# Loading two attention pairs before the branch, and an MLP step's activation inside attention's last steps

## The chip, the cores and the metric

The kernel runs on one core of a Trainium2 chip. The metric is the time of one execution in device microseconds. Before the change it is 683.89 us (median of 3 runs, 683.73 to 685.13).

## What is computed

Banded attention with eight global keys, then two MLPs on its output, everything in float32:

```
# attention: 2 batches, 8 heads, 768 positions, head size 64
scores = q @ k.T / 8 + bias[h]                 # bias = -slope[h] * distance
keep   = (key < n_global) | (0 <= i - key < n_local)       # 8 and 96
a = softmax(where(keep, scores, -1e9))
x = (a @ v)  reshaped to 1536 tokens x 512
# first MLP: 512 -> 2048 -> 512
h = x @ w_in
x = (h * tanh(softplus(h))) @ w_out            # mish
# second MLP: 512 -> 1536 -> 512
xn = x / rms(x) * rms_g
out = (silu(xn @ w_gate) * (xn @ w_val)) @ w_out2
```

## The kernel before

**Branch.** Ahead of the branch come the loads of the two limits, the first loads of attention, and the maps from which the bias is made. All engines then read a flag; with the limits of these inputs they go to `attention_banded`. Four tiles of `room`, which hold the MLP's sums later, hold data for the start of attention.

**Attention.** Heads are worked in pairs. A pair of a batch has 6 units, one for each 128 queries, so there are 48 units and 24 steps of two units; pair n begins with step 3n. A unit meets at most 256 keys. Its operations, with their engines: scores (TensorE, L651), a custom VectorE operation that adds the bias and reduces (L677), the exponential (ScalarE, L690), the inverse sums for two units (VectorE, L701 and L702), scaling (GpSimd, L706), transposes (TensorE, L715), their evacuation (ScalarE, L723), the product with the values (TensorE, L736), and for every third unit the split of the result into a high (ScalarE, L355) and a low half (VectorE, L358).

**Weights.** A weight piece comes as 64-bit words into one of four `stage` tiles (512 KiB; L129). Seven operations make its two halves: `mag` (L161), `clamp` (L167), `b1` (L170), `b2` (L176), `b3` (L182) on VectorE, `hi` and `lo` on GpSimd for the six early pieces (L193, L201), on ScalarE and VectorE for later ones. `mag` of piece i asks for the loads up to piece i, `b3` of piece i for those up to piece i + 3. Pieces 0 to 3 are `w_in`, 4 to 7 `w_out`, 8 and 9 `w_in` again.

**The plan.** In attention each operation has a due time in steps: its step plus the offset in `AT`. The offsets are: scores 0, reduction 0.95 and 1.44, exponential 1.36 and 1.68, inverse sums 2.2, scaling 2.71 and 3.16, transposes 3.29, evacuation 3.87, values 4.65, high split 5.15, low split 5.77 (first and second unit of a step). A piece's operations are due at `CONV_AT[k]` plus the offsets in `AT_CONV`, or `AT_LATE` for pieces 4 and 5. The work of each engine is sorted by due time, and every engine executes its list in this order. A step that stands ahead of another on its engine holds it up. SP issues all DMAs in order as well, except for four loads of the first values, which ScalarE's queue issues.

**Attention's data.** Pair 0 lies in `room` tiles: queries and keys in two halves, values in two halves. Pairs from 1 on go to a pool with two buffers each for queries, keys and values; pair n's load waits for the last use of pair n - 2.

**MLP 1.** It has 32 steps s. A step makes two chunks of 128 hidden columns for 384 tokens: 24 products (L367), then mish: `tanh` of each chunk (L387), a table load and two functions (`cosine`, L391 to L393), `times` (VectorE, L396), a high split (L493) and a low split (L497). The sums of a step (18 products with `w_out`, L419) are put off into `pend` and issued by `flush(0)` of the next step's mish, behind the next step's products. The first four chunks (`ahead`) are multiplied among attention's last steps; `mish1(0, ...)` follows attention, `mish1(1, ...)` opens `mlps`. Each mish also handles the weight pieces begun by the one before; `begin(2)` at the end of the first starts pieces 6 and 7, five VectorE operations each.

Of the kernel before, what the change touches and what calls it, by code (L numbers as in the profile page):

```python
# [17 lines left out]
P = 128  # L18
B, H, S, D = 2, 8, 768, 64
NT = S // P  # L20
# [6 lines left out]
TB = BT // P  # L27
# [22 lines left out]
CONV_AT = (3.0, 7.0, 11.0, 14.5, 21.2, 22.2)  # L50
# [10 lines left out]
def tile_attention_mish_swiglu(  # L61
# [163 lines left out]
    q_first = room[2][:, 0:S]  # L225
    k_first, v_first = (
        room[i][:, 0 : (2 * NT - 1) * P].rearrange("p (n c) -> p n c", c=P) for i in (3, 0)
    )
    maps = room[1]

    def tiles_v(v_t, b, p, own=slice(0, NT), queue=None):


        queue = queue or sp
        vp = v[b][:, p * P : (p + 1) * P]
        vr = vp.rearrange("(t r) e -> r t e", r=P)
        queue.dma_start(v_t[:, own, :], vr[:, own, :])
        n, last = max(own.start - 1, 0), own.stop - 1
        win = slice(NT + n, NT + last)
        for r in (slice(GLOBAL_MAX, 64), slice(64, P)):  # L240
            queue.dma_start(v_t[r, win, :], vr[r, n:last, :])  # L241
        queue.dma_start(
            v_t[0:GLOBAL_MAX, win, :],
            vp[0:GLOBAL_MAX].rearrange("r (o e) -> r o e", o=1).to_broadcast(
                (GLOBAL_MAX, last - n, P)
            ),
        )

    for m in range(2):
        tok = slice(m * BT, (m + 1) * BT)  # L250
        own, win = slice(m * TB, (m + 1) * TB), slice(NT + (m and 2), NT + 2 + 3 * m)
        sp.dma_start(q_first[:, tok], qT[0, 0][:, tok])
        sp.dma_start(k_first[:, own, :], kT[0, 0][:, own, :])
        sp.dma_start(k_first[:, win, :], kT[0, 0][:, win, :])
# [11 lines left out]
    tiles_v(v_first, 0, 0, slice(0, TB), act)  # L266
# [235 lines left out]
    def mish1(s, mish):  # L502

        blk, cs = s // 2 % NBLK, chunks(s)
# [21 lines left out]
        begin(BEGUN1[s])  # L526

# [64 lines left out]
    def attention_banded():  # L592
        fresh()
        mm = [mm_bank() for _ in range(4)]
        with ExitStack() as st:
# [15 lines left out]
            def load_v(b, p):  # L611
                v_t = qk.tile([P, 2 * NT - 1, P], F32, tag="v", name=nm("v"))
                tiles_v(v_t, b, p)
                vs[b, p] = v_t

            qs[0, 0], ks[0, 0], vs[0, 0] = q_first, k_first, v_first
            load_qk(0, 1)
            tiles_v(vs[0, 0], 0, 0, slice(TB, NT))
            sp.dma_start(gcol, rms_g)
            conv_prefetch(2)  # L620

# [177 lines left out]
            for h in range(2, H):  # L799
                add("DVE", 1.5 * h - 1.3, ("BIAS", h), [("BIAS", h - 1)],  # L800
                    lambda h=h: make_bias(h))
            for n in range(2, B * NPAIR):
                add("SP", 3 * n - 3.9, ("LOADQK", n), [("QK", NT * (n - 1) - 1)],
# [197 lines left out]
```

## Time and profile before

| | |
|---|---|
| median of 3 runs | 683.89 us |
| the profiled execution | 687.29 us |
| its span | 685.5 us |
| TensorE busy in the span | 660.5 us (96%) |
| VectorE | 448.6 us (65%) |
| ScalarE | 379.5 us (55%) |
| GpSimd | 65.5 us (10%) |

The profile is of one execution. The busy time of TensorE includes matmuls at a lower granted clock, so a busy slice is not yet a fast one; its clock has two levels, 2.4 GHz (shown as 1.00) and 1.2 GHz (0.50). A line of the timeline gives the start, the duration, engine, source line, operation, the tiles, the count, and in brackets how long the engine was idle before it and what ended that. The idle time of an engine that is not the bottleneck costs nothing.

### The profile page before, as it was taken

The numbers are of one execution on the slowest core, as the hardware profiler recorded it, in microseconds if no ns is written. First come the engines' busy times: TensorE is split into PE (matmuls) and PEld (weight loads), VectorE is DVE, ScalarE is ACT, GpSimd is POOL, SyncE is SP. The second block draws the span as 40 slices with busy tenths as digits, with TensorE's granted clock in tenths as the row PEclk, the third lists the DMA queues.
The fourth block names the chain that finished last, engine by engine and source line by source line (L and its number), as shares of the span: only waits on it lengthen the run. The fifth ranks groups of instructions, "written<-read, shape, count | busy, mean of one in ns | idle before, by whom it ended". The sixth has DMA issues, their size and how long they took to land.

```text
span 685.5 us, 9837 instructions
## 1 busy us (share of the span) xinstructions
PE 660.5 (96%) x3712; PEld 589.5 (86%) x3712; DVE 448.6 (65%) x1029; ACT 379.5 (55%) x716; POOL 65.5 (10%) x124
## 2 busy tenths in 40 slices
PE   6979997999999999999999999999999999999996
PEld 3657786999999999999878999999999999999995
DVE  4768857887788778877777787882467873232222
ACT  3969968888888888888888322321122221111211
POOL 1547870000000000000000000000000000000000
PEclk9798998999999999999999999999999999999999
DMA  7775632222212212221112122221013200010011
GB/s 232 218 235 180 204 103 63 92 93 65 71 63 92 80 63 68 86 62 63 62 62 62 45 79 94 80 74 32 1 61 99 87 1 0 1 47 12 35 47 51
DMA packets 26727, 54.19 MB, mean 79 GB/s; under 512 B 2608, under 2 KB 14640, under 8 KB 26672
## 3 DMA queue, kind: packets, MB, share of 16 engines
q1 hardware_dynamic: 25968, 53.16, 24.3%
q8 instruction: 31, 0.51, 0.3%
q10 hardware_dynamic: 704, 0.33, 0.2%
q14 instruction: 24, 0.20, 0.1%
HBM read 50.34 MB, written 3.15 MB: 78 GB/s over the span
## 4 chain that ended last, share of the span: by engine, by line
PE 85%; ACT 5%; DVE 5%; DMA 2%; issue 1%; SPq 1%; DVEq 0%; POOL 0%; POOLq 0%
PE mm L367 45%; PE s L419 31%; PE s L736 3%; PE s L715 3%; PE mm L651 3%; DMA stage<-in_w_in_dram 2%; DVE x L431 1%; ACT junk L465 1%; DVE d L396 1%; ACT e L690 1%; ACT L391 1%; ACT L387 1%; PE s L448 1%; SPq L241 0%; DMA lim_i<-in_n_global_dram 0%
## 5 line engine op out<-in xcount | busy, mean ns | idle before, releaser
L367 PE MATMUL mm<-hl,w 128*128 128x384 f32 x1920 | 349.4, 336 | 0.0
L367 PEld LDWEIGHTS mm<-hl,w 128*128 128x128 f32 x1920 | 336.8, 188 | 7.1 <-issue 0.5
L419 PE MATMUL s<-w,g 128*128 128x512 f32 x1008 | 249.2, 397 | 6.8 <-issue 5.0
L419 PEld LDWEIGHTS s<-w,g 128*128 128x128 f32 x1008 | 188.6, 190 | 45.2 <-issue 5.2
L557 ACT ACTIVATE r<-mm 128x384 f32<-128x384 f32 x48 | 23.5, 490 | 128.6 <-PE mm L367 128.6
L558 DVE TENSOR_TENSOR r<-r,mm 128x384 f32<-128x384 f32 x48 | 26.4, 549 | 65.9 <-ACT r L557 65.9
L431 DVE TENSOR_TENSOR x<-x,s 128x512 f32<-128x512 f32 x60 | 40.2, 687 | 40.2 <-PE s L419 40.2
L493 ACT ACTIVATE g<-r 128x384 fp32r<-128x384 f32 x48 | 25.2, 525 | 71.5 <-DVE r L558 71.5
L396 DVE TENSOR_TENSOR d<-d,mm 128x384 f32<-128x384 f32 x64 | 32.5, 549 | 35.1 <-ACT d L393 35.1
L690 ACT ACTIVATE e<-e,s 128x256 f32<-128x256 f32 (+1 forms) x96 | 46.2, 502 | 11.5 <-DVE s L677 11.5
L706 POOL TENSOR_SCALAR e<-e,s 128x256 f32<-128x256 f32 (+1 forms) x96 | 47.8, 515 | 35.1 <-ACT e L690 10.7
L182 DVE SCALAR_TENSOR_TENSOR bits<-stage,bits 128x512 int32<-128x512 int32 x68 | 47.4, 697 | 2.1
L176 DVE SCALAR_TENSOR_TENSOR bits<-stage,bits 128x512 int32<-128x512 int32 x68 | 47.3, 695 | 2.1
L493 ACT ACTIVATE g<-d 128x384 fp32r<-128x384 f32 x64 | 33.5, 526 | 24.1 <-DVE d L396 22.6
L497 DVE TENSOR_TENSOR g<-r,g 128x384 fp32r<-128x384 f32 x48 | 26.8, 559 | 28.4 <-ACT g L493 28.4
L201 DVE TENSOR_TENSOR w<-bits,w 128x512 fp32r<-128x512 f32 x62 | 42.7, 688 | 0.0
L391 ACT ACT_TABLE_LOAD x32 | 41.1, 1283 | 0.6
L387 ACT ACT_TABLE_LOAD x31 | 39.8, 1283 | 0.5
L677 DVE CUSTOM_DVE_ANT_0 e<-mm,bias 128x256 f32<-128x256 f32 (+1 forms) x96 | 33.8, 392 | 8.2 <-PE s L715 7.3
L197 ACT ACTIVATE w<-bits 128x512 fp32r<-128x512 f32 x62 | 38.2, 616 | 0.0
L387 ACT ACTIVATE d<-mm 128x384 f32<-128x384 f32 x64 | 30.2, 491 | 12.0 <-PE mm L367 10.5
L161 DVE TENSOR_SCALAR bits<-stage 128x512 int32<-128x512 int32 x68 | 28.8, 424 | 11.2 <-DMA stage<-in_w_in_dram 11.2
(79 smaller groups left out, 472.4 us busy)
## 6 DMA issues: line engine op xcount, KB each, us to landing
stage<-in_w_out_dram SPq DMA_DIRECT2D x28, 512.0 KB, 3.2
stage<-in_w_in_dram SPq DMA_DIRECT2D x16, 512.0 KB, 3.9
stage<-in_w_gate_dram SPq DMA_DIRECT2D x12, 512.0 KB, 3.4
stage<-in_w_val_dram SPq DMA_DIRECT2D x12, 512.0 KB, 3.4
k<-in_kT_dram SPq DMA_DIRECT2D x7, 704.0 KB, 4.4
out_dram<-x SPq DMA_DIRECT2D x12, 256.0 KB, 2.1
q<-in_qT_dram SPq DMA_DIRECT2D x7, 384.0 KB, 5.1
v<-in_v_dram SPq DMA_DIRECT2D x7, 384.0 KB, 4.6
```

Source lines behind the costliest of these rows:

```text
L176: dve.scalar_tensor_tensor(self.bits, self.lw, 29, self.bits, op0=ALU.logical_shift_right, op1=ALU.bitwise_or,)
L182: dve.scalar_tensor_tensor(self.bits, self.hw, -1073741824, self.bits, op0=ALU.bitwise_and, op1=ALU.bitwise_or,)
L201: engine.tensor_tensor(self.wt[:, 1, :], self.fl, self.wt[:, 0, :].bitcast(F32), op=ALU.subtract)
L367: pe.matmul(ps[:, 0:BT], w[:, wi, col], xs[kc][:, xi, :], start=kc == 0 and i == 0, stop=kc == NK - 1 and i == 2,)
L387: act.activation(self.t[:, i, :], self.h[i], AF.Tanh, scale=0.5)
L391: act.preload_act_table_set("trig_and_small")
L396: dve.tensor_tensor(self.t[:, i, :], self.t[:, i, :], self.h[i], op=ALU.mult)
L419: pe.matmul(acc[m], gt[:, gi, tok], w[:, wi, :], start=c % 4 == 0 and i == 0, stop=c % 4 == 3 and i == 2,)
L431: dve.tensor_tensor(y, y, acc[m], op=ALU.add)
L493: act.activation(gt[:, 0, :], x, AF.Copy)
L690: act.activation(e, e, AF.Exp, scale=-1.0, bias=s[:, 0, u % 2, j : j + 1], accum_out=s[:, 1, u % 2, j : j + 1],)
L706: pool.tensor_scalar(e, e, es[u // 2][1][:, 3, u % 2, j : j + 1], 0.0, op0=ALU.mult, op1=ALU.add,)
```

## The change

- The loads of pair 1's queries and keys go ahead of the branch, into the `room` tiles 2 and 0. Pair 0's values go from `room` tile 0 into the pool; they are loaded whole, from SP, behind the branch. The helper `tiles_v` with its halves and its choice of queue goes away.
- The order of loads on SP behind the branch becomes: piece 0, pair 0's values, `rms_g`, pair 2's queries and keys, piece 1, pair 1's values, pieces 2 and 3. Pair 3's queries and keys are next and wait for nothing; values from pair 2 on wait for the values product of pair n - 2.
- `CONV_AT` moves the early pieces 0 to 3 later by 1.6, 1.0, 0.4 and 0.2 steps.
- Of the 16 `ahead` products, those of chunks 0 and 1 come closer together (0.12 steps apart instead of 0.23), those of chunks 2 and 3 spread over 25.0 to 27.3 steps.
- The mish of chunks 0 and 1 becomes planned work: `tanh` at 25.2 and 25.7, `cosine` at 25.95, `times` at 27.0, the splits at 27.3 and 27.5. Behind the plan come `begin(2)` for pieces 6 and 7, and `sums_later`, which puts off the sums of step 0; `mish1(1, ...)` then issues them.

```diff
--- before.py
+++ after.py
@@ -47,7 +47,7 @@
     "HI": (5.15, 5.16), "LO": (5.77, 5.66),
 }
 
-CONV_AT = (3.0, 7.0, 11.0, 14.5, 21.2, 22.2)
+CONV_AT = (4.6, 8.0, 11.4, 14.7, 21.2, 22.2)
 AT_CONV = dict(mag=-0.53, clamp=0.96, b1=3.89, b2=6.09, b3=7.15, hi=7.69, lo=8.79)
 AT_LATE = dict(mag=2.5, clamp=3.0, b1=3.4, b2=4.0, b3=4.5, hi=5.0, lo=5.5)
 
@@ -222,36 +222,20 @@
 
 
     room = [xypool.tile([P, TB * DM], F32, tag="xy", name=nm("x")) for _ in range(NBLK)]
-    q_first = room[2][:, 0:S]
-    k_first, v_first = (
+    q_first = [room[2][:, i * S : (i + 1) * S] for i in range(2)]
+    k_first = [
         room[i][:, 0 : (2 * NT - 1) * P].rearrange("p (n c) -> p n c", c=P) for i in (3, 0)
-    )
+    ]
     maps = room[1]
-
-    def tiles_v(v_t, b, p, own=slice(0, NT), queue=None):
-
-
-        queue = queue or sp
-        vp = v[b][:, p * P : (p + 1) * P]
-        vr = vp.rearrange("(t r) e -> r t e", r=P)
-        queue.dma_start(v_t[:, own, :], vr[:, own, :])
-        n, last = max(own.start - 1, 0), own.stop - 1
-        win = slice(NT + n, NT + last)
-        for r in (slice(GLOBAL_MAX, 64), slice(64, P)):
-            queue.dma_start(v_t[r, win, :], vr[r, n:last, :])
-        queue.dma_start(
-            v_t[0:GLOBAL_MAX, win, :],
-            vp[0:GLOBAL_MAX].rearrange("r (o e) -> r o e", o=1).to_broadcast(
-                (GLOBAL_MAX, last - n, P)
-            ),
-        )
 
     for m in range(2):
         tok = slice(m * BT, (m + 1) * BT)
         own, win = slice(m * TB, (m + 1) * TB), slice(NT + (m and 2), NT + 2 + 3 * m)
-        sp.dma_start(q_first[:, tok], qT[0, 0][:, tok])
-        sp.dma_start(k_first[:, own, :], kT[0, 0][:, own, :])
-        sp.dma_start(k_first[:, win, :], kT[0, 0][:, win, :])
+        sp.dma_start(q_first[0][:, tok], qT[0, 0][:, tok])
+        sp.dma_start(k_first[0][:, own, :], kT[0, 0][:, own, :])
+        sp.dma_start(k_first[0][:, win, :], kT[0, 0][:, win, :])
+    sp.dma_start(q_first[1], qT[0, 1])
+    sp.dma_start(k_first[1], kT[0, 1])
 
     small = cpool.tile([P, 28], F32, tag="small", name="small")
     half, mhalf = small[:, 0:1], small[:, 1 : 1 + TB]
@@ -263,7 +247,6 @@
     dve.memset(mhalf, -0.5)
     dve.memset(half_pi, HALF_PI)
     act.activation(primed, half, AF.Exp)
-    tiles_v(v_first, 0, 0, slice(0, TB), act)
     ones = room[1][:, 10 * P : 12 * P].bitcast(BF16)
     dve.memset(ones, 1.0)
     dve.memset(least[:, 0:1], 1.0)
@@ -501,7 +484,6 @@
 
     def mish1(s, mish):
 
-        blk, cs = s // 2 % NBLK, chunks(s)
         for i in range(2):
             mish.tanh(i)
         do_one(between)
@@ -524,6 +506,10 @@
             piece("lo")
         do_one(ends)
         begin(BEGUN1[s])
+        sums_later(s, gt)
+
+    def sums_later(s, gt):
+        blk, cs = s // 2 % NBLK, chunks(s)
 
         def later():
             def done(m):
@@ -609,15 +595,31 @@
                 qs[b, p], ks[b, p] = q_t, k_t
 
             def load_v(b, p):
+
+
                 v_t = qk.tile([P, 2 * NT - 1, P], F32, tag="v", name=nm("v"))
-                tiles_v(v_t, b, p)
+                vp = v[b][:, p * P : (p + 1) * P]
+                vr = vp.rearrange("(t r) e -> r t e", r=P)
+                sp.dma_start(v_t[:, 0:NT, :], vr)
+                for r in (slice(GLOBAL_MAX, 64), slice(64, P)):
+                    sp.dma_start(v_t[r, NT:, :], vr[r, 0 : NT - 1, :])
+                sp.dma_start(
+                    v_t[0:GLOBAL_MAX, NT:, :],
+                    vp[0:GLOBAL_MAX].rearrange("r (o e) -> r o e", o=1).to_broadcast(
+                        (GLOBAL_MAX, NT - 1, P)
+                    ),
+                )
                 vs[b, p] = v_t
 
-            qs[0, 0], ks[0, 0], vs[0, 0] = q_first, k_first, v_first
-            load_qk(0, 1)
-            tiles_v(vs[0, 0], 0, 0, slice(TB, NT))
+            for p in range(2):
+                qs[0, p], ks[0, p] = q_first[p], k_first[p]
+            conv_prefetch(1)
+            load_v(0, 0)
             sp.dma_start(gcol, rms_g)
+            load_qk(0, 2)
             conv_prefetch(2)
+            load_v(0, 1)
+            conv_prefetch(4)
 
             biases = bp.tile([P, H, 3 * P], BF16, tag="bias", name="bias")
             bias, bias0 = biases[:, :, 0 : 2 * P], biases[:, :, 2 * P :]
@@ -799,12 +801,12 @@
             for h in range(2, H):
                 add("DVE", 1.5 * h - 1.3, ("BIAS", h), [("BIAS", h - 1)],
                     lambda h=h: make_bias(h))
+            for n in range(3, B * NPAIR):
+                add("SP", 3 * n - 3.9, ("LOADQK", n),
+                    [("QK", NT * (n - 1) - 1)] if n > 3 else [],
+                    lambda n=n: load_qk(*divmod(n, NPAIR)))
             for n in range(2, B * NPAIR):
-                add("SP", 3 * n - 3.9, ("LOADQK", n), [("QK", NT * (n - 1) - 1)],
-                    lambda n=n: load_qk(*divmod(n, NPAIR)))
-            for n in range(1, B * NPAIR):
-                add("SP", 3 * n + (0.7 if n > 2 else -2.4), ("LOADV", n),
-                    [("PV", NT * (n - 1) - 1)] if n > 2 else [],
+                add("SP", 3 * n + 0.7, ("LOADV", n), [("PV", NT * (n - 1) - 1)],
                     lambda n=n: load_v(*divmod(n, NPAIR)))
             pieces = [Piece(k) for k in range(NW_EARLY)]
             for k, piece in enumerate(pieces):
@@ -813,15 +815,25 @@
                     add("POOL" if op in ("hi", "lo") else "DVE", at, (op, k),
                         [("lo", k - 3)], lambda piece=piece, op=op: piece(op))
 
+
             for j in range(4 * NK):
-                add("PE", ns - 0.1 + 0.23 * j, ("AHEAD", j),
+                add("PE", ns - 0.1 + (0.12 * j if j < 8 else 1.1 + 0.33 * (j - 8)), ("AHEAD", j),
                     [("TTR", nu - 4 + k, c) for k in range(2 + 2 * (j >= 8)) for c in range(2)]
                     + [("lo", j % NK)],
                     lambda j=j: ahead(j))
+            mish, gt = [], []
+            add("ACT", ns + 1.19, ("MISH",), [("AHEAD", 4)], lambda: mish.append(Mish(first[0:2])))
             for c in range(2):
-                add("ACT", ns + 1.3 + 0.7 * c, ("TANH", c),
-                    [("AHEAD", 4 * c + 3)], lambda c=c: mish_first[0].tanh(c))
-            mish_first = []
+                add("ACT", ns + 1.2 + 0.5 * c, ("TANH", c), [("AHEAD", 4 * c + 3)],
+                    lambda c=c: mish[0].tanh(c))
+                add("DVE", ns + 3.0 + 0.01 * c, ("TIMES", c), [("COSINE",)],
+                    lambda c=c: mish[0].times(c))
+                add("ACT", ns + 3.3 + 0.01 * c, ("HIGH", c), [("TIMES", c)],
+                    lambda c=c: gt.append(split_hi(mish[0].t[:, c, :])))
+                add("DVE", ns + 3.5 + 0.01 * c, ("LOW", c), [("HIGH", c)],
+                    lambda c=c: split_lo(gt[c], mish[0].t[:, c, :]))
+            add("ACT", ns + 1.95, ("COSINE",), [("TANH", 0), ("TANH", 1)],
+                lambda: mish[0].cosine())
 
 
             names = {w[3] for w in work}
@@ -836,13 +848,12 @@
             while any(queues.values()):
                 w = min(q[0] for q in queues.values() if q and ready(q[0]))
                 queues[w[2]].pop(0)
-                if w[3] == ("TANH", 0):
-                    mish_first.append(Mish(first))
                 w[5]()
                 done.add(w[3])
             for piece in pieces:
                 piece.rest()
-            mish1(0, mish_first[0])
+            begin(BEGUN1[0])
+            sums_later(0, gt)
         mlps(1, Mish(first[2:4]))
 
 
```

## Rows read from the trace of the kernel before

**Rows 1.** The page, part 2: busy tenths in 40 slices, and the clock.
```profile
PE   6979997999999999999999999999999999999996
...
PEclk9798998999999999999999999999999999999999
```

**Rows 2.** Chain of waits in order of time: start us, us, what; whole kernel.
```profile
11.31 5.50 DMA stage<-in_w_in_dram
...
84.94 1.06 PE mm L651 x8
...
102.75 1.02 PE s L736 x16
103.78 4.99 issue
108.77 6.74 PE s L419 x18
...
123.79 4.18 PE mm L367 x24
127.98 4.12 PE s L419 x18
```

**Rows 3.** Timeline, 11 to 25 us, TensorE's scores and transposes, VectorE's first piece.
```profile
14.32 1.18 PE L651 MATMUL mm<-k,q 64*128 64x128 f32 x8 [2.92 <-DMA q<-in_qT_dram]
...
16.83 0.43 DVE L161 TENSOR_SCALAR bits<-stage 128x512 int32<-128x512 int32 x1 [5.31 <-DMA stage<-in_w_in_dram]
...
18.78 2.42 PE L651 MATMUL mm<-k,q 64*128 64x256 f32 x8 [1.80 <-DVE s L677]
...
21.13 1.97 PE L715 MATMUL s<-ident,e 128*128 128x128 f32 x8
...
24.51 1.41 PE L651 MATMUL mm<-k,q 64*128 64x256 f32 x8
```

**Rows 4.** Pair 1's queries: issue (timeline, SP), then KB and us to landing.
```profile
6.96 0.44 SPq L608 DMA_DIRECT2D q<-in_qT_dram  x1
...
q<-in_qT_dram SPq DMA_DIRECT2D x1, 384.0 KB, 7.2
```

**Rows 5.** Stretches: engines' busy us (instructions), TensorE's clock, DMA share, GB/s.
```profile
0.00:9.00 9.00, 6.38 (x28) 2.68 (x28) 4.94 (x36) 2.94 (x9) 1.08 (x8) 1.00 0.66 182
...
4.00:6.00 2.00, 1.66 (x8) 0.61 (x7) 0.86 (x7) 0.00 (x0) 0.00 (x0) 1.00 1.05 376
9.00:25.00 16.00, 11.28 (x60) 7.49 (x58) 8.06 (x47) 10.49 (x40) 6.05 (x14) 0.68 0.98 295
...
25.00:26.00 1.00, 1.00 (x9) 0.56 (x8) 0.00 (x0) 0.79 (x4) 1.00 (x3) 0.95 0.93 182
...
30.00:42.00 12.00, 12.00 (x130) 9.19 (x126) 9.49 (x49) 12.00 (x45) 7.89 (x17) 1.00 0.46 153
```

**Rows 6.** Timeline, 36 to 71 us: scores of steps 9, 11 and 18, a piece.
```profile
36.58 0.93 PE L651 MATMUL mm<-k,q 64*128 64x128 f32 x8
...
42.17 1.13 PE L651 MATMUL mm<-k,q 64*128 64x256 f32 x8
...
46.86 0.43 DVE L161 TENSOR_SCALAR bits<-stage 128x512 int32<-128x512 int32 x1 [5.89 <-DMA stage<-in_w_in_dram]
...
70.02 0.93 PE L651 MATMUL mm<-k,q 64*128 64x128 f32 x8
```

**Rows 7.** Timeline, 94 to 127 us, ScalarE and VectorE.
```profile
94.56 1.08 ACT L723 ACTIVATE pt<-s 128x512 f32<-128x512 f32 x2 [1.36 <-PE s L715]
...
104.35 0.56 DVE L358 TENSOR_TENSOR hl<-s,hl 128x384 fp32r<-128x384 f32 x1 [3.21 <-ACT hl L355]
...
106.59 0.93 ACT L393 ACTIVATE d<-d,small 128x768 f32<-128x768 f32 x1
...
109.65 0.42 DVE L161 TENSOR_SCALAR bits<-stage 128x512 int32<-128x512 int32 x1
...
126.90 1.02 DVE L497 TENSOR_TENSOR g<-d,g 128x384 fp32r<-128x384 f32 x2
```

## Prediction

> **What bounds the kernel now.** I read the slices first, then the chain of waits, then the timeline around each place where the chain leaves TensorE. TensorE is busy in 9 tenths of nearly every slice; the thin or slow ones are the second to fourth and the one around 110 us, where the clock row shows 7 as well [rows 1]. The chain shows two holes in the first 115 us: 5.50 us for a weight stage issued at 11.31, and 4.99 us without work at 103.78, after which the first 18 sums take 6.74 us where later ones take 4.12 [rows 2]. The timeline adds a third, 5.89 us of idle VectorE up to 46.86 [rows 6]. From 113 us on the chain is TensorE's, so what is won before stays won unless a helper then falls short.
>
> Steps are counted as in the plan: step i holds units 2i and 2i+1, pair n begins with step 3n, QK(i) are the scores of step i.
>
> *Hole 1.* VectorE sits idle 5.31 us until 16.83, because `mag` of piece 0 (due 2.47) stands ahead of the reductions of step 2 (due 2.95) and its stage lands only then [rows 3]. Beside it TensorE waits 2.92 us, from 11.4 to 14.32, for pair 1's queries. QK(5) comes at 24.51.
>
> *Hole 2.* VectorE waits there for the stage of piece 2: `b3` of piece 0 (due 10.15) asks for that load only 0.32 steps ahead of `mag` of piece 2 (10.47), and the request then queues behind a load of values.
>
> *Hole 3.* The first mish's table load and its two functions on ScalarE start only behind the last high split of attention, whose low half begins at 104.35, and end at 107.52 [rows 7].
>
> The work between is ScalarE's: QK(18) at 70.02 to QK(23) at 84.94, which is 2.98 us a step [rows 2, 6].
>
> **Start of attention.** All early bytes go through one queue, so I date landings by bytes. By 9.0 us 182 GB/s x 9.0 = 1638 kB had moved, and 295 GB/s from there to 25 [rows 5]. A load lands some time after its own bytes could be through: pair 1's queries (issued 6.96, 7.2 us to landing, so 14.2 [rows 4]) end at 2556 kB of the order, when 1638 + 5.2 x 295 = 3172 kB had moved: 616 kB late. Piece 0's stage (11.31 + 5.50 = 16.8 [rows 2]) ends at 3475 kB, moved 3939: 464 kB late. I take 500 kB.
>
> The new order on SP is pair 0 (1088 KiB), pair 1 (1088), piece 0 (512), pair 0's values (704), pair 2's keys and queries (1088), piece 1 (512), pair 1's values (704), pieces 2 and 3 (1024), pair 3's keys and queries (1088). By (end + 500 - 1638)/295 + 9 they land at: pair 1 12.7, piece 0 14.5, values 0 16.9, pair 2 20.7, piece 1 22.5, values 1 24.9, pieces 2 and 3 28.5, pair 3 32.2. The first values left ACT's queue (320 KiB = 328 kB there), so SP alone may have moved up to 328 kB less by 9.0, 0 to 1.1 us; I add 0.3, because SP is blocked in that time for only some of it. Pair 1 is then there at 13.0 instead of 14.2.
>
> Now the two waits. `mag` of piece 0 goes to 4.07, behind the reductions of steps 2 and half of 3, which need the transposes of step 0. These follow QK(3), 13.0 + 1.1 + 0.9 = 15.0; the stage is there at 14.5 + 0.3 = 14.8, so the 5.31 us go. What is late next is pair 1: QK(3) at 13.0. Steps 3 to 5 then take what steps 9 to 11 take, 42.17 - 36.58 = 5.59 us [rows 6], so QK(5) stands at 18.6 instead of 24.51. The first values product comes after QK(3), transposes 0, QK(4) and transposes 1, about 1.1 each, so near 17.3; its data is there at 16.9 + 0.3 = 17.2. That cover is thin: each us later costs a us. From QK(5) to QK(9) 36.58 - 24.51 = 12.07 us, so QK(9) is due at 30.7 - but pair 3's data, now behind two more stages, lands at 32.5. ScalarE, which sets the pace, works about a step behind the scores and so takes up the first of that wait; I allow 0.7 us, an estimate between nothing and the whole. QK(9) counts as 31.8 against 36.58: **4.8 us won**; ends 3.1 (below) and 5.9 (no wait for pair 3).
>
> At this place the DMA: Bandwidth & Descriptors page of the Trainium skill ("Issuing engines are not separate DMA queues") says that a second issuing queue saves only issue time, because the same 16 engines move the bytes. The row at 4 to 6 us shows 376 GB/s with both queues feeding, the stretch with SP alone 295 [rows 5]. By the rule the 0.3 us would be nothing, and the whole 666.1.
>
> **Middle.** Four stages exist and all four are loaded by 28.5 to 28.8; `mag` of pieces 1 and 2 stand at 7.47 and 10.87 steps, about 26 and 37 us. From QK(11) at 42.17 to QK(18) at 70.02 are 27.85 us; seven steps at 2.98 are 20.9. **7.0 us won** (the 5.89 us idle, and the half clock that follows it); ends 6.0 (some of it was work caught up later) and 7.1. By the same dating pair 2's values land at 35.0 against a need at 36.7, and pair 4's keys and queries at 38.8 against QK(12) at 40.7. The other edits of the SP order (pair n's loads wait for pair n-2, as before) cost nothing by the same margins. ACT loses four DMA issues that nothing waited for.
>
> **End of attention.** From 84.94 to the last values at 102.75 the chain holds TensorE's pieces without a wait of 0.1 us (18 pieces, the first and the last in [rows 2]), and the change only reorders its work: chunks 0 and 1 move to 23.9 to 24.74 in the plan, chunks 2 and 3 spread to 27.31. The last values then end at the same distance, 103.78 on the old clock. Mish moves among them: two tanh, then table load and two functions on ScalarE (104.35 to 107.52, 3.2 us [rows 7]) between the evacuations of steps 22 and 23. The evacuation of step 22 began at 94.56; two more chunk steps (three products each, 4.18/8 = 0.5 us) now stand ahead of its transposes, so it ends near 94.6 + 1.0 + 1.1 = 96.7 or, with tanh of chunk 1 ahead of it, 97.2. The block ends at 100.4, the evacuation of step 23 at 101.5; its values begin at 102.75. That is 1.3 us of cover; were it gone, up to 1.9 us would be late. `times`, high and low splits end about 103.5. So the sums start at 103.85 with no idle and at the high clock: 4.99 + (6.74 - 4.12) = 7.6 us leave TensorE.
>
> But VectorE gives some back. It runs with no idle from 109.65 (first op of piece 6) to the low split of the third mish at 126.90 [rows 7]. In the changed kernel that run starts behind the last low split of attention, 104.35 + 0.56 = 104.91: 4.74 us earlier, not 7.6. The low split's first half ends at 126.90 + 0.55 - 4.74 = 122.7; the sums that need it (127.98 before [rows 2]) can start two matmuls (0.46) earlier, at 122.2. TensorE would be there at 103.85 + 2 x (4.12 + 4.18) = 120.5 [rows 2] and waits 1.8. **5.7 us won**; ends 4.5 (evacuations late) and 7.4 (VectorE not the limit).
>
> **Sum.** 4.8 + 7.0 + 5.7 = 17.5 us. The profiled execution took 687.29 us, its span 685.5; changed: 669.8 and 668.0. The median of the runs is 3.4 us under the profiled one; taking the same gain off it: 683.89 - 17.5 = **666.4 us**.
>
> **Rivals.** (1) *Half clock in the ramp.* Today the clock is at 1.2 GHz for most of 15 to 25 us after TensorE sat idle, back at 25.05, 6.3 us after gapless work began at 18.78 [rows 3, 5]. If QK(3) at 13.0 meets the low clock too, QK(4) costs 2.42 instead of 1.13, and two blocks of transposes (1.97 for eight at the low clock, half of that at the high one) 0.7 and 0.9 more, rounded down to 2.8 us as the clock falls late. QK(5) at 21.4, pair 3 no longer late: 3.1 won there, 668.1. For: idle from 11.4 to 13.0. Against: half as much idle as now. The TensorE: Matmul & The Clock Gate page of the Trainium skill (Part 4) says that transposes don't count as busy work for the clock in the way matmuls do; by that the ramp, a third transposes, would stay slow and the time be this rival's 668.1. The stretch from 30 to 42 us, with the same mix and no idle, is at 1.00 throughout [rows 5], so the trace doesn't bear the rule out there.
> (2) *Loads late.* With 616 kB and the full 328 kB: QK(3) 14.2, pair 3 33.8, 3.5 won, 667.7. At 250 GB/s instead of 295, pair 4 is late as well (44 us, QK(12) at 43.5 for 49.44, and 2.7 us of the later loss): 5.9 + 2.7 + 5.7 = 14.3, 669.6. For: piece 0 and values 0 now share the fullest stretch.
> (3) *The end does not do what it says*: the mish is not ready at the last values, since tanh of chunk 1 waits for eight chunk steps and ScalarE works in order. Then idle returns and only the clock part, 2.6, stays: 669.5.
> (4) *More:* no wait for pair 3, no VectorE limit: 5.9 + 7.0 + 7.4 = 20.3, 663.6.
> (5) *Slower.* TensorE stays at the low clock through attention, because small idle gaps now come evenly. A step costs 2.42 + 1.97 + about 2.0 for the values (taken as the transposes') = 6.4 us at 1.2 GHz [rows 3] against 2.98: 3.4 more. From 17.5/3.4, over five more slow steps than now, it is slower; ten more give 700. Against: all steps from 26 to 42 us were at the high clock.
>
> **How the numbers follow.** Forecast 0.50, (1) 0.15, (2) 0.14, (3) 0.08, (4) 0.09, (5) 0.04. About 0.2% (1.4 us) is what a measurement of this kernel can tell from no change. Faster 0.95; same 0.02 and slower 0.03 come out of (5). Range 662.5 to 673: from (4) less 1, to (2) and (3) together (671 to 673).
>
> **What would show it.** VectorE's first piece op with no idle over 1 us ahead of it; QK(5) at 18 to 19 us; QK(9) waiting 1 to 2 us for `k` or `q`; no wait of VectorE for a stage near 35 to 45; QK(23) near 73; L419 following the last L736 within 0.3 us at clock 1.00; then some 2 us in which the third block of sums waits for L497. Wrong would be: clock 0.50 between 13 and 20 (rival 1), the first L736 waiting for `v` (2), L736 of step 23 or L419 waiting for ScalarE (3).

## The result, and the profile of the changed kernel

| | before | after | after / before |
|---|---|---|---|
| median of 6 runs each, us | 684.80 | 668.62 | 0.9761 [0.9746, 0.9776] |
| profiled execution | 687.29 | 668.87 | |
| its span | 685.5 | 667.1 | 18.4 less |
| TensorE busy in it | 660.5 (96%) | 653.8 (98%) | |

The change takes 16.2 us off the median; 17.5 was forecast, and 666.4 us for 668.62. On the page, TensorE and its clock in 40 slices (answers [rows 1]):

```profile
PE   8999999999999999999999999999999999999996
...
PEclk9999999999999999999999999999999999999999
```

The 7s of the third slice and of the one near 110 us are gone, the first slice is an 8 for a 6, and the clock row has no slice under 9 any more (before: a 7 and two 8s [rows 1]). Where the time went is read from the timeline of TensorE (start, duration, operation, count, idle time before and what ended it), start to middle of attention:

```profile
11.61 0.93 PE L653 MATMUL mm<-x,x 64*128 64x128 f32 x8 [0.21 <-DMA x<-in_kT_dram]
...
17.05 0.44 PE L738 MATMUL s<-pt,v 128*64 128x128 f32 x4 [0.49 <-DMA v<-in_v_dram]
17.41 1.13 PE L653 MATMUL mm<-x,x 64*128 64x256 f32 x8
...
29.73 0.93 PE L653 MATMUL mm<-k,q 64*128 64x128 f32 x8 [0.44 <-DVE s L703]
...
35.30 1.13 PE L653 MATMUL mm<-k,q 64*128 64x256 f32 x8
...
56.19 0.93 PE L653 MATMUL mm<-k,q 64*128 64x128 f32 x8
...
71.12 1.14 PE L653 MATMUL mm<-k,q 64*128 64x256 f32 x8
```

These are QK(3), the first product with the values, QK(5), QK(9), QK(11), QK(18) and QK(23); L653 was L651 [rows 3, 6]. VectorE's first piece operation, 5.31 us idle in [rows 3], now has no wait in brackets:

```profile
14.00 0.66 DVE L161 TENSOR_SCALAR bits<-stage 128x512 int32<-128x512 int32 x1
```

The end of attention on TensorE: last values, then the first, second, third and fifth block of sums (L402 was L419):

```profile
89.27 1.09 PE L738 MATMUL s<-pt,v 128*64 128x128 f32 x16
90.29 4.40 PE L402 MATMUL s<-w,g 128*128 128x512 f32 x18
...
98.71 4.26 PE L402 MATMUL s<-w,g 128*128 128x512 f32 x18
...
108.29 0.73 PE L402 MATMUL s<-w,g 128*128 128x512 f32 x2 [1.13 <-ACT g L476]
109.27 3.92 PE L402 MATMUL s<-w,g 128*128 128x512 f32 x16 [0.24 <-DVE g L480]
...
125.58 0.73 PE L402 MATMUL s<-w,g 128*128 128x512 f32 x2
126.56 3.93 PE L402 MATMUL s<-w,g 128*128 128x512 f32 x16 [0.24 <-DVE g L480]
```

The 4.99 us without work and the slow 6.74 us block of [rows 2] are gone; the sums follow the values at once, at 4.40 us. The same kernel was profiled a second time with the last experiments ("again"). Starts of the same work in us, and what each profile of the changed kernel has won by then:

| | before | after | won | again | won |
|---|---|---|---|---|---|
| QK(5) | 24.51 | 17.41 | 7.1 | 18.01 | 6.5 |
| QK(11) | 42.17 | 35.30 | 6.9 | 36.67 | 5.5 |
| QK(18) | 70.02 | 56.19 | 13.8 | 57.17 | 12.9 |
| QK(23) | 84.87 | 71.12 | 13.7 | 72.09 | 12.8 |
| first sums | 108.77 | 90.29 | 18.5 | 91.26 | 17.5 |
| sixth block of sums | 152.72 | 134.51 | 18.2 | 135.45 | 17.3 |
| last block of sums | 674.91 | 656.67 | 18.2 | 657.64 | 17.3 |
| end of the span | 685.5 | 667.1 | 18.4 | 666.7 | 18.8 |

So the start won 5.5 to 6.9 us, the middle 7.0 to 7.4, the end 4.5, and behind the sixth block nothing more happens but the very end of the span.

### The profile page after: what moved, and what is told of

Read it like the earlier page. It is cut to its first block, busy times and chain, and to the rows that moved or that the text cites. A ratio compares the mean times of both kernels' runs of the same rounds, so it can differ in the third digit from the quotient of the medians.

```text
span 667.1 us, 9833 instructions
## 1 busy us (share of the span) xinstructions
PE 653.8 (98%) x3712; PEld 582.9 (87%) x3712; DVE 450.6 (68%) x1029; ACT 378.4 (57%) x716; POOL 68.0 (10%) x124
## 4 chain that ended last, share of the span: by engine, by line
PE 82%; DVE 8%; ACT 5%; DMA 2%; issue 1%; SPq 0%; DVEq 0%; POOL 0%; POOLq 0%
PE mm L350 44%; PE s L402 29%; PE s L717 3%; PE s L738 3%; PE mm L653 3%; DMA v<-in_v_dram 1%; DVE x L414 1%; DVE d L379 1%; DVE bits L176 1%; ACT junk L448 1%; ACT L374 1%; ACT L370 1%; DVE bits L182 1%; DVE g L480 1%; DVE w L201 1%
## 5 line engine op out<-in xcount | busy, mean ns | idle before, releaser
L402 PE MATMUL s<-w,g 128*128 128x512 f32 x1008 | 247.6, 394 | 3.4 <-ACT g L476 2.1
L402 PEld LDWEIGHTS s<-w,g 128*128 128x128 f32 x1008 | 186.5, 188 | 42.4 <-DVE g L480 3.6
L476 ACT ACTIVATE g<-r 128x384 fp32r<-128x384 f32 x48 | 25.2, 525 | 71.6 <-DVE r L544 71.6
L379 DVE TENSOR_TENSOR d<-d,mm 128x384 f32<-128x384 f32 x64 | 32.5, 549 | 35.3 <-ACT d L376 35.3
L708 POOL TENSOR_SCALAR e<-e,s 128x256 f32<-128x256 f32 (+1 forms) x96 | 49.3, 530 | 22.8 <-ACT e L692 9.7
L480 DVE TENSOR_TENSOR g<-d,g 128x384 fp32r<-128x384 f32 x64 | 32.6, 551 | 0.7 <-ACT g L476 0.7
```

The lines of the kernel that those rows point to most:

```text
L402: pe.matmul(acc[m], gt[:, gi, tok], w[:, wi, :], start=c % 4 == 0 and i == 0, stop=c % 4 == 3 and i == 2,)
L476: act.activation(gt[:, 0, :], x, AF.Copy)
L480: dve.tensor_tensor(gt[:, 1, :], x, gt[:, 0, :].bitcast(F32), op=ALU.subtract)
L708: pool.tensor_scalar(e, e, es[u // 2][1][:, 3, u % 2, j : j + 1], 0.0, op0=ALU.mult, op1=ALU.add,)
```

## The experiments

Times are medians beside runs of the kernel before on the same chip; the ratio is to those. "Above" and "under" compare with the 668.62 us of the changed kernel. Its own ten runs reach from 667.67 to 669.74 us, so that steps of 0.8 to 1.4 us are small beside the spread, and what causes them is read from the traces. Diffs are against the changed kernel unless it says otherwise, and lines left out are marked by dots.

**The end as before.** The plan of the last steps and the first mish go back to the old form, the loads stay:

```diff
-                add("PE", ns - 0.1 + (0.12 * j if j < 8 else 1.1 + 0.33 * (j - 8)), ("AHEAD", j),
+                add("PE", ns - 0.1 + 0.23 * j, ("AHEAD", j),
...
-            begin(BEGUN1[0])
-            sums_later(0, gt)
+            mish1(0, mish_first[0])
```

> The changed kernel, but with the end of attention as before: the four chunks evenly spaced, mish of chunks 0 and 1 behind the plan. Theory (the end is worth what VectorE lets through): the idle of about 5 us and the half clock return, but the waits of the third and fifth block of sums for VectorE go, so 4.6 us more, 673.2. Rival (the end is worth all of TensorE's hole): 7.6 us more, 676.2.

Measured: 672.96 us (672.18 to 674.88), 0.9814 [0.9796, 0.9833]: 4.3 above the changed kernel. The hole is back, at its old size, with the slow block behind it:

```profile
97.45 7.11 PE L402 MATMUL s<-w,g 128*128 128x512 f32 x18 [5.00 <-issue]
```

From QK(23) to the sixth block of sums it takes 4.85 us more than the changed kernel (68.24 for 63.39), and not the 4.7 + 2.7 us by which its first sums are late and slow: behind them, up to the sixth block, it has no waits of the sums for VectorE, which the changed kernel has. The profiled execution (674.88 us) is the slowest of the four: it has lost time in the ramp as well, which this edit doesn't touch (its row stands at rival 1 below).

**Two stages instead of four.** Only the last prefetch behind the branch is taken out:

```diff
             load_v(0, 1)
-            conv_prefetch(4)
```

> The changed kernel without the early load of pieces 2 and 3, which are asked for by the last operation of piece 0 or by the first of piece 2, as before. Theory (hole 2 is that request): VectorE waits 5 us or more for the stage of piece 2 near 35 to 40 us and 6 to 7 us are lost, 675. Rival (ScalarE sets the pace and VectorE's wait is absorbed, while the later data of pair 3 come sooner): at most 2 us more, 670.6.

Measured: 672.57 us (671.83 to 673.00), 0.9813 [0.9793, 0.9832]: 4.0 above. VectorE's wait for a stage, and behind it TensorE's, with scores at the low clock (1.88 us, where they take 0.93):

```profile
39.55 0.43 DVE L161 TENSOR_SCALAR bits<-stage 128x512 int32<-128x512 int32 x1 [4.36 <-DMA stage<-in_w_in_dram]
...
41.33 1.88 PE L652 MATMUL mm<-k,q 64*128 64x128 f32 x8 [3.04 <-DVE s L678]
```

QK(11) to QK(18) takes 25.56 us, 4.7 more than in the changed kernel. The hole of [rows 6] returns, but as 4.36 us of waiting and not 5.89. Why it is smaller is not shown; an earlier request is not the reason, for with the new due times `mag` of piece 2 (10.87) asks for its stage itself, ahead of `b3` of piece 0 (11.75). The 4.0 us are less than my theory gave and more than the rival.

**Four stages in the kernel before**, the same edit the other way round (against the kernel before):

```diff
             sp.dma_start(gcol, rms_g)
-            conv_prefetch(2)
+            conv_prefetch(4)
```

> The kernel before, with pieces 2 and 3 loaded right behind pieces 0 and 1. Theory (hole 2 is the late request, its 5.89 us of idle VectorE and the half clock behind it go): 7.0 us less than before, minus up to 1 us because pair 2's data come later, 678.5. Rival (the half clock comes from the start and stays, or pair 2's data open a new hole): at most 4 us less, 681.

Measured: 680.39 us (678.58 to 681.77), 0.9930 [0.9904, 0.9956], 4.9 under the kernel before on its chip. Steps 11 and 18:

```profile
41.92 1.13 PE L651 MATMUL mm<-k,q 64*128 64x256 f32 x8
...
62.73 0.93 PE L651 MATMUL mm<-k,q 64*128 64x128 f32 x8
```

The stretch is 20.81 us long, for 27.85 in [rows 6]: the middle is worth 7.0 in the trace by itself, while the median moved 4.9. Those two numbers differ by about as much as the 18.4 and 16.2 of the whole change. So the trace bears the theory out, while the median is near the rival's 681.

**Piece 0 due early again.**

```diff
-CONV_AT = (4.6, 8.0, 11.4, 14.7, 21.2, 22.2)
+CONV_AT = (3.0, 8.0, 11.4, 14.7, 21.2, 22.2)
```

> The changed kernel with piece 0 due at 3.0 again instead of 4.6, the loads as changed. Theory (hole 1 was VectorE's list, the load order is the smaller half): its first operation stands ahead of the reductions of step 2 again and waits for the stage until about 13.2, 1.9 us of idle VectorE, 1.5 to 2 us more, 670.3. Rival (pair 1's data and the values decide the ramp): within 0.5 us, 668.6.

Measured: 670.74 us (669.09 to 670.78), 0.9777 [0.9760, 0.9795]: 2.1 above. VectorE waits for the stage, TensorE for VectorE, and QK(4) then runs at 1.2 GHz:

```profile
14.27 0.43 DVE L161 TENSOR_SCALAR bits<-stage 128x512 int32<-128x512 int32 x1 [2.77 <-DMA stage<-in_w_in_dram]
...
16.22 2.01 PE L653 MATMUL mm<-x,x 64*128 64x256 f32 x8 [1.89 <-DVE s L679]
```

**Only piece 0 late, in the kernel before** (against the kernel before):

```diff
-CONV_AT = (3.0, 7.0, 11.0, 14.5, 21.2, 22.2)
+CONV_AT = (4.6, 7.0, 11.0, 14.5, 21.2, 22.2)
```

> The kernel before with one number changed: piece 0 of the weights is due at step 4.6 instead of 3.0, so that VectorE no longer stands waiting for its stage at 11.5 to 16.8 us; the order of the loads stays. Theory (two of three causes remain: pair 1's queries still land at 14.2, and with piece 0 later the stage of piece 2 is asked for later still, so the second hole stays or grows): QK(5) at 20 to 21.5 instead of 24.5, VectorE's wait near 47 us not under 5.9 us, the whole 2 to 3 us under the kernel before, about 682.3. Rival (the due time alone carries the start's gain, and the second hole is not lengthened): 5 us or more under, 680 or less.

Measured: 683.26 us (680.81 to 684.62), 0.9976 [0.9962, 0.9990]: 1.4 under the kernel before. The wait of 11.5 to 16.8 is gone, the one for pair 1's queries stays, and so does the second hole, at its full size:

```profile
14.47 1.66 PE L651 MATMUL mm<-k,q 64*128 64x128 f32 x8 [2.90 <-DMA q<-in_qT_dram]
...
43.74 0.43 DVE L161 TENSOR_SCALAR bits<-stage 128x512 int32<-128x512 int32 x1 [5.87 <-DMA stage<-in_w_in_dram]
```

QK(5) stands at 21.96. One due time alone is a small part of the gain, less than the theory's 2 to 3 us; it needs pair 1 and the stages.

**Pair 1 behind the branch**, ahead of piece 0, instead of ahead of it:

```diff
-    sp.dma_start(q_first[1], qT[0, 1])
-    sp.dma_start(k_first[1], kT[0, 1])
...
+            sp.dma_start(q_first[1], qT[0, 1])
+            sp.dma_start(k_first[1], kT[0, 1])
             conv_prefetch(1)
```

> The changed kernel with pair 1's queries and keys loaded as the first loads behind the branch instead of ahead of it; all other loads as changed. Theory (the branch costs SP about 1 us, and the order does the rest): pair 1 lands about 1.1 us later, at 12.7, the first values as much later, 0.8 to 1.1 us more, 669.6. Rival (the place ahead of the branch is the main part of the start's 6.9 us): 3 us or more, 672.

Measured: 669.46 us (668.73 to 670.43), 0.9774 [0.9746, 0.9803]: 0.8 above. SP issues the queries at 5.47 instead of 4.47, and QK(3) comes at 13.39. So the place ahead of the branch is worth about a microsecond at the most; the runs (668.73 to 670.43) overlap with the changed kernel's. What brings QK(3) from 14.32 [rows 3] to 13.39 here is not pair 1's place in the order either: in the kernel before, it was the first load behind the branch too. But its two loads were issued at 6.58 and 6.96 there, and here at 5.47 and 5.84, with no loads on ScalarE's queue beside them (next run).

**ScalarE's early loads put back.** The old first half of pair 0's values is loaded once more on ScalarE's queue, 328 kB that nobody uses, ahead of the branch:

```diff
     act.activation(primed, half, AF.Exp)
+    act.dma_start(early[:, 0:TB, :], vr[:, 0:TB, :])
...
```

> The changed kernel plus four loads of 320 KiB from ScalarE's queue ahead of the branch, as the first values were loaded before (into a tile that nothing reads here). Theory (a second queue holds SP up): SP pauses between 3.5 and 5 us as before, pair 1 is there near 13.5 instead of 11.6, scores of step 5 near 19.3 instead of 17.4, 1.5 to 2 us more, 670.4. Rival (only the bytes count, 328 kB at 333 GB/s): no pause of SP and 1.0 us more, 669.6.

Measured: 669.95 us (669.15 to 670.34), 0.9774 [0.9747, 0.9802]: 1.3 above. SP's sixth and seventh load, from this kernel's timeline:

```profile
3.05 0.43 SPq L234 DMA_DIRECT2D x<-in_qT_dram  x1
4.98 0.33 SPq L235 DMA_DIRECT2D x<-in_kT_dram  x1
```

In the changed kernel the seventh is issued at 3.52, without a pause; in the kernel before at 5.04, after a pause as long as here. The loads behind it are 1.4 us late and more, QK(3) stands at 13.84, and QK(4) meets the low clock (2.08 us).

**More bytes ahead of pair 3**, 786 kB that nobody uses:

```diff
             conv_prefetch(4)
+            for r in range(2):
+                more = dpool.tile([P, 2, BT], F32, tag="d", name=nm("more"))
+                sp.dma_start(more.rearrange("p a b -> p (a b)"), qT[1, r])
```

> Two loads that nobody uses, 393 kB each, stand on SP's queue just ahead of pair 3's keys and queries in the changed kernel. Theory (pair 3 is there early, by the bytes: 333 GB/s from 9 us on and no lag put it at about 28 us, against QK(9) at 29.7, so its cover is some 1.8 us): the 786 kB take 2.4 us of the queue, QK(9) then waits about 0.6 us for k or q, and the time is 0.3 to 0.8 above the changed kernel's 668.6, near 669.2. Rival (the prediction's own dating, pair 3 at 32.5 with no cover at all): QK(9) moves by the whole 2.4 us and the time by 1.7 to 2.4, to 670.3 to 671.0.

Measured: 670.90 us (670.41 to 672.29), 0.9803 [0.9779, 0.9827]: 2.3 above. The rival's time, but QK(9) stands only 1.2 us later than in the first profile of the changed kernel, and not 2.4:

```profile
30.96 1.40 PE L656 MATMUL mm<-k,q 64*128 64x128 f32 x8 [2.22 <-DVE hl L341]
32.29 1.54 PE L720 MATMUL s<-ident,e 128*128 128x128 f32 x6
```

The bracket names a VectorE operation that ended at 30.85, by coincidence: pair 3's queries, issued at 22.42 and 8.4 us on their way, land at 30.82. There is no cover, as the wait of 0.44 us in the changed kernel says already. The row alone doesn't tell the added bytes from the spread between executions, for the run with the end as before, with no bytes added, has nearly the same one (at rival 1 below). The times do: all four lie above the ten of the changed kernel. The transposes behind the wait run at the low clock (1.54 us for six, where six take 0.87 in the changed kernel's step 3), and QK(10) comes at 35.22, 4.26 us after QK(9) instead of 2.68. These 1.6 us of low clock, which neither theory priced, are over half of the loss.

**VectorE's pieces 6 and 7 moved into attention's last steps.**

```diff
+            add("DVE", ns + 2.9, ("PIECE", 6), [("COSINE",)], lambda: begin(1))
+            add("DVE", ns + 3.8, ("PIECE", 7), [("PIECE", 6)], lambda: begin(1))
...
-            begin(BEGUN1[0])
             sums_later(0, gt)
```

> The changed kernel with VectorE's ten operations of pieces 6 and 7 brought forward: piece 6 ahead of the first times, in the 2.79 us in which VectorE waits for the cosine, piece 7 ahead of the last low split of attention. Theory (VectorE limits the opening of the first MLP): the waits of the third and the fifth block of sums shrink by 2.0 to 2.6 us in all, 666.2. Rival (ScalarE's table loads limit it): 0 to 0.5 us, 668.4.

Measured: 667.18 us (667.08 to 669.38), 0.9741 [0.9722, 0.9761]: 1.4 under. In the trace the last block of sums is only 0.5 us earlier than in the first profile of the changed kernel (656.20 for 656.67); the rest lies behind it, where executions differ anyway (below). So the rival is nearer. The moved operations ran long beside GpSimd's, but that is not why the third block still waits. VectorE is done with them in time to sit idle for 2.15 us, until ScalarE's function of the second mish ends; from there (96.34, for 96.84 in the changed kernel) it has the two pieces of step 1, the copies and the third mish's `times` to do without a gap:

```profile
82.95 1.60 POOL L201 TENSOR_TENSOR w<-bits,w 128x512 fp32r<-128x512 f32 x1
...
83.33 1.50 DVE L161 TENSOR_SCALAR bits<-stage 128x512 int32<-128x512 int32 x1
...
96.34 1.02 DVE L379 TENSOR_TENSOR d<-d,mm 128x384 f32<-128x384 f32 x2 [2.15 <-ACT d L376]
...
107.80 0.73 PE L402 MATMUL s<-w,g 128*128 128x512 f32 x2 [0.61 <-ACT g L476]
```

**VectorE's extra pieces later.** Two of the six steps that begin two pieces move from 1 and 3 to 4 and 6:

```diff
-BEGUN1 = [1 + (s < 2 or s % 8 == 3) for s in range(NC1 * NBLK // 2)]
+BEGUN1 = [1 + (s in (0, 4, 6, 11, 19, 27)) for s in range(NC1 * NBLK // 2)]
```

> The changed kernel with the two extra weight pieces that steps 1 and 3 of the first MLP begin given to steps 4 and 6, in whose next step VectorE has no copies or additions of sums. Theory (two pieces, three copies and times together are more than VectorE does in one step): the waits ahead of the third block of sums (1.8 us) and the fifth (0.6 us) go, 666.3. Rival (ScalarE's two table loads a step limit it, as bringing pieces 6 and 7 forward gained only 1.5): within 0.7 us, 668.

Measured: 665.29 us (665.00 to 668.24), 0.9718 [0.9694, 0.9743]: 3.3 under, the fastest of all runs. No block of sums waits any more up to 326 us (the short waits from there to 357 us are in the kernel before too, at 346 to 375); third and fifth:

```profile
107.46 4.28 PE L402 MATMUL s<-w,g 128*128 128x512 f32 x18
...
124.07 4.28 PE L402 MATMUL s<-w,g 128*128 128x512 f32 x18
```

From the first to the sixth block it takes 41.64 us, for 44.22 in the changed kernel: 2.6 of the 3.3.

**Both moves of VectorE's work**, the two edits above in one kernel.

> The changed kernel with both moves of VectorE's work at the end of attention: pieces 6 and 7 planned into the last steps of attention, and the extra piece of steps 1 and 3 begun in steps 4 and 6. Theory (with the extra piece later, 665.3, no sums wait for VectorE any more up to 316 us, so there is nothing left to win by the other move): 665.3, within 0.7 of it. Rival (VectorE still holds back the block between 91 and 127 us in some way that the first waits hid): 664.3 or less. In the trace none of the first ten blocks of sums waits for the high or low split under the theory.

Measured: 665.46 us (665.04 to 666.16), 0.9715 [0.9693, 0.9736], from the first to the sixth block 41.64 again. Once these sums don't wait, moving the pieces forward wins nothing, as the theory had it.

**The changed kernel again.**

> The changed kernel itself, beside the other three. Theory: 668.6 within 0.5, a ratio of 0.976, and the stretch from the last block of sums on TensorE to the end of the span, 10.4 us in its first profile and 8.8 to 9.4 in those of its variants, belongs to an execution and not to the program, so that it can be anything from 8.8 to 10.6 here. Rival: the last stretch is the program's own, 10.4 again, and then a part of what a variant won (1.6 us of the 3.3 of the one with the extra piece later) comes from the end of the program and not from the waits of the sums.

Measured: 668.45 us (667.98 to 669.74), 0.9764 [0.9740, 0.9789]. The last stretch, 10.4 us in the first profile, is 9.1 here with the same program: it belongs to the execution. Beside it, both moves together are 3.0 faster, of which 2.4 stand at the last block of sums (655.25 for 657.64).

## Why the prediction was right, and where it was not

**Middle: right.** 7.0 us forecast, 7.0 and 7.4 in the two profiles, 7.0 with four stages alone in the kernel before. The reason holds too: with two stages the wait for the stage returns. Four stages are enough for the whole 7.0; taken out of the changed kernel they cost 4.7, because the wait that returns is the shorter one. (In [rows 1] I read the clock's digit at 110 us as 7; it is 8. The clock's return that I put at 25.05 us stands at 25.10. Nothing rests on either.)

**Start: the right steps, landings dated too late.** The forecast counted 4.8 us; 6.9 and 5.5 came. Four other runs have the same program up to here (the end as before, and the three that move VectorE's pieces), so that six profiles show one and the same start: 4.0 to 6.9 us won at QK(11). Pair 3's queries landed at 29.56 to 31.11 in them, where I had 32.5, and pair 1's keys at 11.4 to 12.5, where I had 13.0. The term that was mis-sized is the rate, 295 GB/s, where the six have 305 to 333 from 9 to 25 us. By the windows of the changed kernel (busy time of the engines, clock, DMA share, GB/s):

```profile
0.00:9.00 9.00, 7.31 (x28) 2.92 (x28) 5.05 (x36) 3.05 (x9) 1.08 (x8) 1.00 0.63 190
...
9.00:25.00 16.00, 15.26 (x135) 10.41 (x132) 12.85 (x72) 15.94 (x61) 10.49 (x23) 1.00 1.08 333
```

With 1710 kB by 9.0 and 333 GB/s the forecast's formula puts pair 3 (ends at 7995 kB) at (7995 + 500 - 1710)/333 + 9 = 29.4; its queries were issued at 21.08 and landed 8.5 us later, at 29.58. In the second profile, with 189 and 305 GB/s, it gives 31.3, and they landed at 22.09 + 8.9 = 31.0. So close a fit is luck: with their own rates the formula is 0.7 us late for the run with the pieces forward (30.3 for 29.56) and 1.2 early for the one with the end as before (29.7 for 30.84). My 295 was the mean of a stretch of the kernel before in which the queue had run thin for a while:

```profile
13.00:17.00 4.00, 2.65 (x14) 1.70 (x14) 0.17 (x1) 0.00 (x0) 0.00 (x0) 0.73 0.79 265
17.00:21.00 4.00, 2.22 (x8) 1.67 (x8) 3.93 (x24) 3.33 (x13) 2.48 (x6) 0.50 1.10 276
21.00:25.00 4.00, 4.00 (x23) 3.21 (x24) 1.89 (x13) 3.74 (x13) 1.93 (x5) 0.50 1.07 325
```

The DMA share of 0.79 beside 1.10 and 1.07 shows it. But that is a part of the error only: without the thin stretch the other three (312 GB/s from 9 to 13 us, 276 and 325) still have a mean of 304, and the fullest has the lowest of the three rates. No row of the kernel before gave the rate that came. Pair 3 is late all the same, as forecast, in most cases less: QK(9) waits 0.44, 0.44, 0.84, 1.21, 1.37 and 2.11 us in the six profiles, where I had 1 to 2, and each time it starts 0.10 to 0.15 us after pair 3's queries land. The second profile's row:

```profile
31.09 0.93 PE L653 MATMUL mm<-k,q 64*128 64x128 f32 x8 [1.21 <-DMA q<-in_qT_dram]
```

**The 0.3 us for SP alone had the wrong sign.** The row was 376 GB/s at 4 to 6 us with both queues; but by 9.0 us the changed kernel had moved no less with SP alone, 190 GB/s for 182 [rows 5]. The run with ScalarE's loads put back shows what the second queue costs: SP's own issue stops for 1.5 us beside it, and the bytes that attention needs come later. So the loads that left ScalarE's queue were a gain and no loss. The DMA: Bandwidth & Descriptors page of the Trainium skill ("Issuing engines are not separate DMA queues") says that issuing from more engines saves nothing but the time of issue; the 190 GB/s agree with it, and here even the time of issue was not saved.

**Thin cover of the first values: the landing right, the cover gone.** Due at 17.3 with data at 17.2, they came at 17.05 after a wait of 0.49 (0.69 in the second profile): pair 1 was there earlier than dated, the values were not. QK(23), forecast near 73, came at 71.1 and 72.1. Rival 2 (loads later still) went the other way.

**Rival 1 (low clock in the ramp) did not happen at QK(3), but its mechanism is real.** The clock is 1.00 in every stretch of both profiles up to 60 us. It fell in the runs where TensorE had waited more: after 1.53 and 1.89 us of idle with piece 0 early, after 1.86 with ScalarE's loads, and after 2.22 with more bytes. And it can fall in the changed kernel's own start, at pair 3. The run with the end as before has the same loads; its queries of pair 3, issued at 20.34, took 10.5 us to 30.84, and the clock from 30 to 34 us is 0.71:

```profile
30.98 1.02 PE L653 MATMUL mm<-k,q 64*128 64x128 f32 x8 [2.11 <-DVE hl L341]
```

QK(10) follows 4.25 us later and not 2.68, so this start won 4.0 us where the others won 5.4 to 6.9. One execution in six met it, and I had priced the low clock only at QK(3). The Part 4 rule of the TensorE: Matmul & The Clock Gate page of the Trainium skill, by which, as I read it, a ramp with so many transposes would stay slow, is not borne out: 1.00 from 9 to 25 us. Rival 5 fell with that row.

**End: the mechanism right, one wait overlooked.** 5.7 forecast, 4.5 measured, the lower bound. The sums follow the values at once and at the high clock, 19.17 us after QK(23) for a forecast of 18.9, so rival 3 is out; rival 4's "no VectorE limit" is out too, for the third block waits for VectorE, 1.13 + 0.24 us and some more between the matmuls: the fourth starts at 117.21, where 98.71 and two undisturbed blocks of 8.31 would give 115.33, 1.9 us. I had 1.8. VectorE's run, from the last low split to the low split that the third block waits for, stands with no gap; its ends:

```profile
90.93 0.56 DVE L341 TENSOR_TENSOR hl<-s,hl 128x384 fp32r<-128x384 f32 x1 [1.49 <-ACT hl L338]
91.41 0.42 DVE L161 TENSOR_SCALAR bits<-stage 128x512 int32<-128x512 int32 x1
...
105.34 1.88 DVE L411 COPY x<-s 128x512 f32<-128x512 f32 x3
...
108.67 1.02 DVE L480 TENSOR_TENSOR g<-d,g 128x384 fp32r<-128x384 f32 x2
```

The failed step is that I stopped there. Steps 1 and 3 both begin two pieces, so the fifth block meets the same run again: 134.51 for 117.21 + 2 x 8.31 = 133.83, 0.7 us more. Beginning the extra pieces later removes both waits, 2.6 us. That edit moves ScalarE's part of these pieces too, but ScalarE was not the limit: it sat idle for 2.79 us ahead of the third block's high split, until VectorE's `times` ended:

```profile
107.72 1.05 ACT L476 ACTIVATE g<-d 128x384 fp32r<-128x384 f32 x2 [2.79 <-DVE d L379]
```

**From the profile to the median: failed.** The terms add up to 17.5, and the profiles have 17.3 to 18.2 up to the last block of sums, the start's excess and the end's lack nearly cancelling, which is luck. But the median moved 16.2, because the step "taking the same gain off the median" assumed that the slower profiled execution is slow in parts that the change doesn't touch. It was 2.5 us above the median of before (684.80), the changed one 0.25 above its own. Every comparison with that one profile says 2 to 3 us more than the medians: 18.4 and 16.2 here, 7.0 and 4.9 with four stages, 4.7 and 1.4 with piece 0 late (spans of 678.5 and 680.8 for 685.5). In that profile the clock is low for more than a moment only from 9 to 25 us (0.68 on average), 46 to 60 (0.76) and 103 to 128 (0.86), all of them stretches that the change works on. And the executions of the kernel before differ by the clock: of the 34 beside the experiments the 16 with a mean clock of 0.983 or less took 686.0 us on average, the 18 above that 684.2, and the profiled one has 0.981, the lowest that any has. This points to a slow part that lay where the change took effect, so that the profiled gain is more than the gain of a typical run; no experiment shows it. The split of the 2 us over the three stretches stays open; from 9 to 25 us two other orders of the old start show 0.79 for 0.68.

## What to carry to other kernels

Date a transfer by the bytes ahead of it in its queue, but give the date the spread that executions show, here 1.5 us for the same loads; a transfer whose cover is within that spread should count as late in some of them. When a wait on one engine is removed, follow the next busy engine through all the blocks that have the same pattern, not only to its first wait. And check a gain read from one profile against how far that execution lay from its median, and against whether what made it slow is what the change removes.

## What the runs showed of the hardware

- Two issuing queues can hold each other up: with four loads on ScalarE's queue, SP's issue paused from 3.48 to 4.98 us; without them it went on every 0.47 us.
- VectorE's shift of 128x512, 0.42 us alone, took 1.50 beside GpSimd's two-input subtraction, and ended at 84.83, 0.28 us after that had ended (82.95 + 1.60 = 84.55). The SBUF — State Buffer page of the Trainium skill ("SBUF: two separate sides") says that GpSimd and some forms of VectorE operations share a port pair, which the one that starts first holds for a whole instruction while the other is blocked. The rows agree; that this shift is of such a form no run shows.
- A fall of the clock adds to the wait ahead of it: with 2.22 us of idle before QK(9), the step behind it took 4.26 us instead of 2.68, and with 2.11 us 4.25. After 1.79 us of idle before QK(3), with pair 1 behind the branch, and after 1.21 and 1.37 before QK(9) it did not fall.
- The busy share of the DMA engines doesn't give the rate: at a share of 1.08 and 1.09 the same loads of the same program moved at 333 and 305 GB/s from 9 to 25 us in two executions, and in the kernel before a stretch at 1.10 had 276 where one at 1.07 had 325.
- From the start of the last block of sums to the end of the span it took 8.8 to 10.6 us, 10.4 and 9.1 with the same program.
